# One form of score product for all 24 pairs of heads, and a remade order of tasks, in an attention and mixture-of-experts kernel

## The chip, the cores and the metric

The kernel runs on one core of one Trainium2 chip. Its time is the device time of one execution in microseconds (us), taken as the median of several runs. The core has a matrix engine (TensorE, in the rows PE, its weight loads PEld), a vector engine (VectorE, DVE), a scalar engine (ScalarE, ACT), a third elementwise engine (GpSimd, POOL) and a queue engine from which most transfers are started (SyncE, SP). Each engine works through its own instructions in the order in which they were written, and waits for the others by semaphores.

## What is computed

Four batches of 448 tokens with 12 heads of 64 columns pass through attention, a dense layer, and a layer of 8 experts of which each token takes one:

```python
q_n, k_n = rmsnorm(q, g_q), rmsnorm(k, g_k)
attn = softmax(q_n @ k_n.T / 8)             # per batch and head, 448 x 448
x = (attn @ v)                              # 1792 tokens x 768
x1 = square(maximum(x @ w_in, 0)) @ w_out   # 768 -> 2048 -> 768
e = argmax(x1 @ w_gate); p = softmax(x1 @ w_gate)[e]; o = sigmoid(x1 @ w_output_gate)[e]
out = p * o * (maximum(x1 @ w1[e], 0) @ w2[e])   # 768 -> 1024 -> 768
```

The inputs are float32. TensorE takes them as pairs of shorter numbers: each operand is split into a high and a low part, and a product a·b is made as high·high + high·low + low·high. Splitting costs one cast or scaled copy (the high part) and one subtraction (the low part) for each operand, on ACT, DVE or POOL.

## The kernel before

**Tiling.** The 12 heads of a batch are taken as 6 pairs. Four batches by six pairs are 24 pairs of heads, numbered b and p; in tile names `qk2_3_0` is tile 0 of batch 2, pair 3. A pair has 128 rows of head columns (64 for each head) and 448 tokens, cut into four chunks of 112.

**Steps of a pair.** `prepare` makes the normalised q and k (`nrm`, on POOL by L330 or on DVE by L331), transposes them on PE into PSUM (`qkps`, L576) and splits them into the tiles `qk`. `scores` makes for one chunk of queries both heads' scores (`sps`, PE), their negated maximum (`nm`, DVE, L664) and the exponential (`p`, ACT, L667). `turn` transposes the exponentials on PE (`pps`, L681), splits them (`pT`, ACT L317 and DVE L688) and multiplies with v (`av`, PE, L699 or L694). `combine` divides by the sum (`r`, `rb`, `rps`, L711 to L722) and joins the heads (`xs`, DVE, L732 and L734). When the six pairs of a batch are done their rows are split (`x`), and the first half of the dense layer can run for that batch: 16 blocks f of 18 products each (`hps`, L765), 288 products a batch. These 1152 products need only x and the weights `win`, so they fill PE between the attention steps of the next batches. The second half (`yps`, L1040), the routing (L1075 to L1258) and a first block of the first expert (L1343 to L1402) follow; from L1445 on the experts run in an order written out by hand.

**Two forms of scores.** For the first seven pairs (`halves`, L413, NHALF = 7) q and k are split over all 128 rows by four instructions of 128x448 (L583, L585, L589, L591), and a head's scores of a chunk are three products over its own 64 rows (L655), one task for each head. For the other 17 pairs each head's high and low part are stacked to 128 rows, which takes eight instructions of 64x448 (L599, L602 on ACT; L606, L610 on DVE) and two copies from one half of the rows to the other (kind `kd`, L317, L318 or L320), 5 tiles rather than 4; a chunk is then one 128-row product per head (L641, a task each) and one 64-row product per head (L649, one task for both).

**The order.** All of it up to L1442 is put down as tasks in a plan (class `Plan`, L84). A task has an engine, a cost, a priority, the buffers that it reads and writes, and perhaps other engines that may take it. `order` places tasks one after the other, by priority, into the first gap of their engine, with a latency between engines (`LAT`, L88), and the instructions are then written in the order of the planned starts. `ALT` (L243) says which other engines may take a kind of task, and at what addition to its priority and wait; `SHIFT` (L255) adds to the priorities of kinds of tasks. So a change of these numbers moves instructions on every engine, though none is added. PSUM has six banks for `qkps`, `sps`, `pps` and `rps` together (`Slots(6)`, L522), and there are eight places for the exponentials.

## Time and profile before

| | us |
|---|---|
| median of three runs | 1207.39 (1204.85 to 1207.52) |
| span of the profiled execution | 1204.1 |
| first score products of the kernel | 19.7 |
| first product of the dense layer (`hps`, batch 0) | 126.9 |
| last `av` product of batch 1 | 241.95 |
| last `av` product of batch 3 | 484.4 |
| last `hps` product | 578.3 |
| first product of the experts' hand-written part | 869.6 |

The profiled execution's span runs from its first to its last instruction; its own time is the span and the little that lies around it, and the median of the three runs is 3.3 us above the span. The mean granted clock of TensorE is 0.984 of full speed. PE is busy for 93% of the span, DVE 63%, ACT 51%, POOL 36%.

### The profile page before, as it was taken

To read this page: it belongs to the slowest core of one execution; us is meant where nothing else is said; L and a number is where in the kernel's file an instruction comes from. 1 tells how busy PE (TensorE), PEld (TensorE's weight loads), DVE (VectorE), ACT (ScalarE), POOL (GpSimd) and SP (SyncE) were. 2 spreads that over 40 slices of the span, in tenths; PEclk is the share of its full clock that TensorE was granted. 3 is DMA by queue.
4 is the path that set the end of the run, shared out by engine and by line. 5 is a ranking of instruction groups with operands and counts; after the bars stand their busy time and mean duration, and the time that the engine had idled before them with its cause. 6 is when DMAs were issued, how large, how long until landed. Compare 5 with 4: busy or idle time off the path is not lost.

```text
span 1204.1 us, 17242 instructions
## 1 busy us (share of the span) xinstructions
PE 1123.9 (93%) x6070; PEld 953.1 (79%) x6070; DVE 759.0 (63%) x1229; ACT 619.6 (51%) x1235; POOL 438.4 (36%) x437
## 2 busy tenths in 40 slices
PE   2999999999999999999999999999989878999997
PEld 2666777878777887998888989898879767897876
DVE  6999999968888688147787253443552566135662
ACT  4788878767776677234442222231252555133551
POOL 5657756575433431243222000013142444114431
PEclk9899999999999999999999999999999988999999
DMA  9933222233212110168533323273464486307601
GB/s 248 284 106 88 85 85 70 69 115 93 70 47 69 62 32 24 54 193 300 185 105 88 101 62 100 62 228 101 144 208 190 142 308 229 133 26 267 229 33 32
DMA packets 84755, 152.57 MB, mean 127 GB/s; under 512 B 10071, under 2 KB 63063, under 8 KB 84608
## 3 DMA queue, kind: packets, MB, share of 16 engines
q1 hardware_dynamic: 81152, 135.44, 36.0%
q0 software_dynamic: 3456, 15.34, 3.5%
q8 instruction: 71, 1.16, 0.4%
q14 instruction: 76, 0.62, 0.2%
HBM read 124.83 MB, written 26.79 MB: 126 GB/s over the span
## 4 chain that ended last, share of the span: by engine, by line
PE 63%; DVE 15%; issue 7%; ACT 6%; DMA 5%; POOL 2%; DVEq 0%; SPq 0%; POOLq 0%; ACTq 0%; another core or an unknown queue 0%
PE yps L1040 15%; PE hps L765 12%; PE hps L1486 9%; PE yps L1531 6%; PE av L699 5%; PE pps L681 4%; PE sps L641 2%; PE sps L649 2%; DVE w1hl L1503 2%; ACT w1hl L1501 2%; DVE pT L688 1%; DVE wout L325 1%; PE qkps L576 1%; DVE nm L664 1%; ACT wout L317 1%
## 5 line engine op out<-in xcount | busy, mean ns | idle before, releaser
L765 PE MATMUL hps<-x,win 128*128 128x448 f32 x1152 | 282.1, 377 | 0.9 <-ACT g L774 0.8
L1040 PE MATMUL yps<-gh,wout 128*128 128x448 f32 x1152 | 245.4, 368 | 2.8 <-ACT wout L317 2.4
L765 PEld LDWEIGHTS hps<-x,win 128*128 128x128 f32 x1152 | 211.7, 189 | 28.4 <-issue 11.1
L1040 PEld LDWEIGHTS yps<-gh,wout 128*128 128x128 f32 x1152 | 213.4, 188 | 22.7 <-ACT wout L317 2.8
L1486 PE MATMUL hps<-w1hl,xT 128*128 128x512 f32 x564 | 141.3, 400 | 14.2 <-DVE w1hl L1503 10.6
L1531 PE MATMUL yps<-w2hl,hT 128*128 128x384 f32 x752 | 144.0, 348 | 0.0
L667 ACT ACTIVATE p<-sps,nm 112x448 f32<-112x448 f32 x192 | 120.5, 635 | 35.5 <-DVE nm L664 34.0
L1486 PEld LDWEIGHTS hps<-w1hl,xT 128*128 128x128 f32 x564 | 103.7, 189 | 41.6 <-DVE w1hl L1503 15.4
L1531 PEld LDWEIGHTS yps<-w2hl,hT 128*128 128x128 f32 x752 | 134.4, 195 | 0.3 <-DVE hT L1479 0.2
L664 DVE TENSOR_REDUCE nm<-sps 112x1 f32<-112x448 f32 x192 | 111.6, 616 | 22.1 <-PE sps L649 20.0
L699 PE MATMUL av<-pT,v 112*128 112x448 f32 x356 | 116.1, 400 | 3.7 <-DVE pT L688 3.4
L688 DVE TENSOR_TENSOR pT<-pps,pT 112x448 fp32r<-112x448 f32 x178 | 105.3, 616 | 9.0 <-ACT pT L317 7.5
L317 ACT CAST pT<-pps 112x448 fp32r<-112x448 f32 x178 | 91.3, 535 | 27.4 <-PE av L699 13.3
L681 PE MATMUL pps<-ident,p 112*112 112x112 f32 x768 | 98.7, 264 | 5.4 <-DVE qk L606 1.6
L681 PEld LDWEIGHTS pps<-ident,p 112*112 112x112 f32 x768 | 82.7, 135 | 21.6 <-ACT p L667 3.3
L317 ACT CAST gh<-gr 128x448 fp32r<-128x448 f32 x64 | 36.1, 565 | 123.4 <-PE yps L1040 106.2
L330 POOL TENSOR_TENSOR g<-g 128x448 f32<-128x448 f32 x57 | 56.5, 991 | 114.8 <-ACT g L774 113.0
L325 DVE TENSOR_TENSOR gh<-gr,gh 128x448 fp32r<-128x448 f32 x64 | 44.6, 697 | 65.4 <-ACT gh L317 65.4
L699 PEld LDWEIGHTS av<-pT,v 112*128 112x128 f32 x356 | 60.6, 190 | 20.8 <-DVE pT L688 6.8
L1503 POOL TENSOR_TENSOR w1hl<-w1r,w1hl 128x1024 fp32r<-128x1024 f32 x14 | 38.2, 2728 | 96.7 <-ACT w1hl L1501 57.3
L1479 DVE TENSOR_TENSOR hT<-tps,hT 128x512 fp32r<-128x512 f32 x30 | 20.7, 690 | 72.4 <-ACT hT L1478 72.4
L330 POOL TENSOR_TENSOR nrm<-raw,rstd 112x512 f32<-112x512 f32 x47 | 51.8, 1123 | 37.2 <-PE qkps L576 27.5
(388 smaller groups left out, 1661.0 us busy)
## 6 DMA issues: line engine op xcount, KB each, us to landing
w2r<-in_moe_w_dram SPq DMA_DIRECT2D x64, 384.0 KB, 8.8
w1r<-in_moe_w_dram SPq DMA_DIRECT2D x42, 512.0 KB, 4.8
gscr<-g SPq DMA_DIRECT2D x64, 224.0 KB, 2.0
gr<-gscr SPq DMA_DIRECT2D x64, 224.0 KB, 2.6
raw<-in_q_dram SPq DMA_DIRECT2D x24, 224.0 KB, 3.1
raw<-in_k_dram SPq DMA_DIRECT2D x24, 224.0 KB, 3.4
vr<-in_v_dram SPq DMA_DIRECT2D x24, 224.0 KB, 2.7
x1s<-row SPq DMA_DIRECT2D x16, 336.0 KB, 3.0
```

Of the source, the lines that this page charges most:

```text
L317: (ACT, act(n, psum), lambda: nc.scalar.copy(dst(), src())),
L330: (POOL, pool(n), lambda: nc.gpsimd.tensor_mul(dst(), a(), b())),
L664: add(DVE, dve(S), pr + 1 + j, lambda j=j: nc.vector.tensor_reduce(nm()[:, j:j + 1], sp[j]()[:CP, :S], AX.X, ALU.max, negate=True), r=[sp[ ...
L667: add(ACT, act(S, True, 2), pr + 3 + j, lambda j=j: nc.scalar.activation(pt[j](), sp[j]()[:CP, :S], AF.Exp, bias=nm()[:, j:j + 1], accum_o ...
L681: nc.tensor.transpose(tp()[:CP, c * CP:(c + 1) * CP], pts[c][j]()[:, kc * CP:(kc + 1) * CP], ident[:CP, :CP])
L688: add(DVE, dve(S), pq + 2, lambda: nc.vector.tensor_sub(ht()[:, 1], tp()[:CP, :S], ht()[:, 0].bitcast(F32)), r=[tp, (ht, 0)], w=[(ht, 1)], ...
L699: add(PE, 187, pq + 3 + x, lambda x=x: nc.tensor.matmul(a_()[:, :S], vt()[:, j, kc, :], ht()[:, x, :], start=kc == 0 and x == 0, stop=kc = ...
L765: add(PE, 188, pr + n_, lambda d=d, x=x, y=y, n_=n_: nc.tensor.matmul(ps()[:, :S], w()[:, x, d * P:(d + 1) * P], x_t[b, d]()[:, y, :], sta ...
L1040: nc.tensor.matmul(ps()[:, :S], w()[:, x, d * P:(d + 1) * P], hl()[:, y], start=f == 0 and i == 0, stop=f == NFC - 1 and i == 2)
L1486: nc.tensor.matmul(hps[n], x, w1hl[d][:, y, n * 512:(n + 1) * 512], start=d == 0 and i == 0, stop=d == NCC - 1 and i == len(prods) - 1,)
L1503: e_.tensor_sub(w1hl[d][:, 1], w1r[d], w1hl[d][:, 0].bitcast(F32))
L1531: nc.tensor.matmul(yps[n][:, :NH], hT[f // HF][:, x, f % HF, :], w2hl[f][:, y, n * NH:(n + 1) * NH], start=f == 0 and i == 0, stop=f == NF ...
```

## The change

Three things change.

**Scores and splits.** All 24 pairs take the 64-row form. The chunk's six products become one task that names the two heads by turns; `halves`, L599 to L610 and the `kd` copies go. Lines move: L576 is L586 after, L583 to L591 are L593 to L601, L641, L649 and L655 are L634, L664 is L640, L667 is L643, L688 is L664, L765 is L741.

**The planner's numbers.** Costs of products go from 187 or 188 to 201 or 203, entering and leaving 64-row products costs 90 and 180, and most latencies change.

**The order.** ALT and SHIFT are replaced, so that tasks change their engine and place.

```diff
     LAT = {
-        (PE, ACT): 200, (PE, DVE): 60, (ACT, PE): 260, (ACT, DVE): 145, (ACT, POOL): 180,
-        (DVE, PE): 210, (DVE, ACT): 130, (DVE, POOL): 160, (POOL, PE): 210, (POOL, ACT): 80,
+        (PE, ACT): 210, (PE, DVE): 205, (ACT, PE): 175, (ACT, DVE): 135, (ACT, POOL): 180,
+        (DVE, PE): 150, (DVE, ACT): 125, (DVE, POOL): 170, (POOL, PE): 170, (POOL, ACT): 80,
...
+    HALF_IN, HALF_OUT = 90, 180
...
-                t["cost"] = clock.run(at, t["cost"], t["rows"])
+                extra = 0
+                if (t["rows"] == 64) != half:
+                    half = not half
+                    extra = self.HALF_IN if half else self.HALF_OUT
+                t["cost"] = clock.run(at, t["cost"], t["rows"]) + extra
...
 ALT = {
+    "norm": {DVE: (-1020, 500)},
...
 SHIFT = {
-    "combine_a": 200, "combine_a1": 3100, "combine_b": 6100, "combine_c": 300, "combine_c0": 1300,
+    "combine_a": 305, "combine_b": 8725, "combine_b1": -3320, "combine_c": 3365, "combine_c1": -12240,
...
-    NQK, NPT, DOUBLE, NHALF = 2, 3, False, 7
+    NQK, NPT, DOUBLE = 2, 3, False
...
-        hl = [new(A, f"qk{i}", NQK, [P, S], F32R, f"qk{b}_{p}_{i}") for i in range(5)]
+        hl = [new(A, f"qk{i}", NQK, [P, S], F32R, f"qk{b}_{p}_{i}") for i in range(4)]
...
-            for j in range(0 if halves(b, p) else 2):
-                add(PE, 187, pr + 0.1 * j, lambda j=j: nc.tensor.matmul(
-                    sp[j]()[:CP, :S], hl[j]()[:, cols], hl[2 + j](), start=True, stop=False),
-                    r=[(hl[j], 0), (hl[j], 1), (hl[2 + j], 0), (hl[2 + j], 1)],
-                    w=[sp[j], (pt[j], 1)], kind=f"scores_a{b}")
-
-            def low():
-                for j in range(2):
-                    own = slice(64 * j, 64 * j + 64)
-                    nc.tensor.matmul(
-                        sp[j]()[:CP, :S], hl[j]()[own, cols], hl[4]()[own], start=False, stop=True)
-
-            def mm(j):
-                own = slice(64 * j, 64 * j + 64)
+            def mm():
+
                 for i_, (x, y) in enumerate(((0, 2), (0, 3), (1, 2))):
-                    nc.tensor.matmul(
-                        sp[j]()[:CP, :S], hl[x]()[own, cols], hl[y]()[own], start=i_ == 0, stop=i_ == 2)
...
+                    for j in range(2):
+                        own = slice(64 * j, 64 * j + 64)
+                        nc.tensor.matmul(
+                            sp[j]()[:CP, :S], hl[x]()[own, cols], hl[y]()[own], start=i_ == 0, stop=i_ == 2)
+
+            add(PE, 600, pr, mm, r=[(hl[x], 0) for x in range(4)], w=sp + [(pt[j], 1) for j in range(2)],
+                rows=64, kind=f"scores_b{b}")
...
-                add(PE, 188, pr + n_, lambda d=d, x=x, y=y, n_=n_: nc.tensor.matmul(
+                add(PE, 203, pr + n_, lambda d=d, x=x, y=y, n_=n_: nc.tensor.matmul(
```

Counted over the attention part of the program (instructions before, after):

| instruction | before | after |
|---|---|---|
| PE score products | 440 | 576 |
| DVE `qk` splits of 64x448 / 128x448 | 68 / 14 | 0 / 48 |
| ACT `qk` splits of 64x448 / 128x448 | 68 / 14 | 0 / 48 |
| copies `qk<-qk`: DVE, ACT, POOL | 16, 10, 8 | 0, 0, 0 |
| `nrm` on DVE, POOL | 1, 47 | 11, 37 |
| `st` products on DVE, POOL | 0, 36 | 6, 30 |
| `v` subtractions on DVE, POOL | 5, 43 | 16, 32 |
| ReLU `g<-hps` on DVE, ACT | 0, 64 | 15, 49 |
| `hps` products ahead of the last `av` of batch 1, 2, 3 | 252, 473, 698 | 207, 406, 694 |
| score chunks behind the last `av` of batch 1 | 48 | 46 |

**Three places in the order.** First PE in the middle of the attention, chunk 1 of batch 2, pair 2 (`sps2_2_1_0` and `sps2_2_1_1` are the two heads' scores; `hps` are the dense layer's products, `x4` at a row's end that so many stand together). Before:

```order
L641 MATMUL sps2_2_0_0_3672<-qk2_2_2_3604,qk2_2_0_3485 112x448
L641 MATMUL sps2_2_1_0_3677<-qk2_2_2_3604,qk2_2_0_3485 112x448
L765 MATMUL hps1_4_3644<-x1_3_3149,win4_1588 128x448 x2
L765 MATMUL hps1_4_3644<-x1_4_3155,win4_1588 128x448 x3
L765 MATMUL hps1_4_3644<-x1_5_3169,win4_1588 128x448 x3
L641 MATMUL sps2_2_0_1_3696<-qk2_2_3_3612,qk2_2_1_3506 112x448
L649 MATMUL sps2_2_0_0_3672<-qk2_2_4_3630,qk2_2_0_3485 112x448
L649 MATMUL sps2_2_0_1_3696<-qk2_2_4_3630,qk2_2_1_3506 112x448
L641 MATMUL sps2_2_1_1_3703<-qk2_2_3_3612,qk2_2_1_3506 112x448
L649 MATMUL sps2_2_1_0_3677<-qk2_2_4_3630,qk2_2_0_3485 112x448
L649 MATMUL sps2_2_1_1_3703<-qk2_2_4_3630,qk2_2_1_3506 112x448
```

The same chunk of the changed kernel, on the same engine:

```order
L741 MATMUL hps1_0_3579<-x1_2_3505,win0_322 128x448
L634 MATMUL sps2_2_1_0_3615<-qk2_2_2_3176,qk2_2_0_3169 112x448
L634 MATMUL sps2_2_1_1_3617<-qk2_2_2_3176,qk2_2_0_3169 112x448
L634 MATMUL sps2_2_1_0_3615<-qk2_2_3_3186,qk2_2_0_3169 112x448
L634 MATMUL sps2_2_1_1_3617<-qk2_2_3_3186,qk2_2_0_3169 112x448
L634 MATMUL sps2_2_1_0_3615<-qk2_2_2_3176,qk2_2_1_3179 112x448
L634 MATMUL sps2_2_1_1_3617<-qk2_2_2_3176,qk2_2_1_3179 112x448
L741 MATMUL hps1_0_3579<-x1_2_3505,win0_322 128x448 x2
```

A chunk's products now stand in one block, and beside them block f = 0 of batch 1's dense layer instead of f = 4: at the same place of the attention 295 filling products have been written instead of 370.

Second DVE near its start, batch 0 (`win0g`, `win0r` are parts of the first weight unit). Before:

```order
L585 SCALAR_TENSOR_TENSOR qk0_1_1_327<-qkps0_1_0_304,gs_75,qk0_1_0_319 128x448
L325 TENSOR_TENSOR win0_300<-win0g_256,win0_300 128x768
L591 TENSOR_TENSOR qk0_1_3_354<-qkps0_1_1_313,qk0_1_2_329 128x448
L688 TENSOR_TENSOR pT0_0_0_0_344<-pps0_0_0_0_322,pT0_0_0_0_344 112x448
L711 TENSOR_SCALAR r0_0_374<-sum0_0_246 112x8
L712 RECIPROCAL r0_0_374<-r0_0_374 112x8
L664 TENSOR_REDUCE nm0_1_0_382<-sps0_1_0_0_370 112x1
```

The changed kernel on the same engine, at the same place:

```order
L347 TENSOR_TENSOR nrm0_1_294<-raw0_1_108,rstd0_154 112x2x4x64
L410 SCALAR_TENSOR_TENSOR win0g_279<-win0r_208,win0g_279 128x768
L458 TENSOR_REDUCE ss1_320<-st1_0_161 112x16
L664 TENSOR_TENSOR pT0_0_0_0_318<-pps0_0_0_0_304,pT0_0_0_0_318 112x448
L595 SCALAR_TENSOR_TENSOR qk0_1_1_344<-qkps0_1_0_312,gs_75,qk0_1_0_331 128x448
L601 TENSOR_TENSOR qk0_1_3_349<-qkps0_1_1_324,qk0_1_2_336 128x448
L687 TENSOR_SCALAR r0_0_361<-sum0_0_250 112x8
L688 RECIPROCAL r0_0_361<-r0_0_361 112x8
L595 SCALAR_TENSOR_TENSOR qk0_2_1_366<-qkps0_2_0_338,gs_75,qk0_2_0_352 128x448
L347 TENSOR_TENSOR nrm0_5_376<-raw0_5_135,rstd0_154 112x2x4x64
L601 TENSOR_TENSOR qk0_2_3_390<-qkps0_2_1_356,qk0_2_2_374 128x448
L347 TENSOR_TENSOR nrm0_5_376<-raw0_5_135,rstd0_154 112x2x4x64
```

Three normalisations stand on DVE that POOL had before; the low part of `win0` has gone from it, and pair 2's splits stand ahead of pair 1's first scores.

Third PE at the end of the planned part, the first expert's first block (`yps0`, `yps1` are its two halves of columns, `xps` the transposes of the next block's rows, `hps0` the next block's first products). Before:

```order
L1392 MATMUL yps0_9215<-w2hl4_8798,hT1_9247 128x384 x3
L1347 MATMUL xps_9007<-ident_68,w1r0_9225 128x128 x6
L1392 MATMUL yps0_9215<-w2hl5_8825,hT1_9247 128x384 x3
L1392 MATMUL yps0_9215<-w2hl6_8850,hT1_9247 128x384 x3
L1392 MATMUL yps0_9215<-w2hl7_8870,hT1_9247 128x384 x3
L1392 MATMUL yps1_9216<-w2hl4_8798,hT1_9247 128x384 x3
```

After:

```order
L1368 MATMUL yps1_9239<-w2hl4_8815,hT1_9231 128x384 x3
L1368 MATMUL yps1_9239<-w2hl5_8842,hT1_9231 128x384 x3
L1368 MATMUL yps1_9239<-w2hl6_8867,hT1_9231 128x384 x3
L1368 MATMUL yps1_9239<-w2hl7_8887,hT1_9231 128x384 x3
L1323 MATMUL xps_9026<-ident_68,w1r0_9252 128x128 x6
```

The six transposes have moved behind the last of the 48 `yps` products; the next block's `hps` products come directly behind them.

## Rows read from the trace of the kernel before

**Rows 1.** Windows: busy us of each engine (instructions), granted clock, DMA share, GB/s.

```profile
30.00:60.00 30.00, 28.47 (x153) 19.09 (x153) 27.89 (x44) 23.74 (x59) 19.06 (x19) 0.85 1.03 285
60.00:127.00 67.00, 63.16 (x395) 43.38 (x396) 65.41 (x117) 59.41 (x146) 43.72 (x53) 1.00 0.32 89
127.00:242.00 115.00, 111.53 (x632) 90.53 (x631) 111.30 (x175) 92.04 (x199) 70.17 (x69) 1.00 0.26 80
242.00:360.00 118.00, 113.48 (x651) 90.78 (x650) 95.39 (x164) 88.20 (x206) 60.31 (x82) 0.99 0.28 83
360.00:485.00 125.00, 122.59 (x720) 99.65 (x719) 98.71 (x170) 87.96 (x208) 41.17 (x50) 1.00 0.14 45
```

**Rows 2.** Chain of work that ended last, shares by line, 240 to 485 us.

```profile
by line: PE hps L765 37.1%; PE av L699 17.0%; PE pps L681 14.6%; PE sps L641 8.5%; PE sps L649 7.4%; PE qkps L576 3.0%; PE rps L722 1.9%; DVE qk L610 1.5%; issue 1.5%; DVE qk L318 1.4%; DVE nm L664 1.0%; POOL stt L499 0.7%; ACT xs L317 0.7%
```

**Rows 3.** Timeline of PE at two marks: start us, us, instruction.

```profile
126.94 0.37 PE L765 MATMUL hps<-x,win 128*128 128x448 f32 x1
...
241.95 0.78 PE L699 MATMUL av<-pT,v 112*128 112x448 f32 x3
```

**Rows 4.** Chain in order of time, score products and transposes on PE: start, us, piece.

```profile
41.88 0.80 PE sps L655 x6
...
44.02 0.79 PE sps L655 x3
...
65.05 1.42 PE sps L655 x12
...
251.03 0.41 PE sps L641 x2
...
252.26 0.39 PE rps L722 x4
...
253.89 0.38 PE sps L649 x2
```

**Rows 5.** Line 649, idle time of PEld before it: cause, us, times.

```profile
  issue: 20.4, 68
```

**Rows 6.** Groups of DVE: shapes, count | busy us, mean ns of one | idle before.

```profile
L606 DVE SCALAR_TENSOR_TENSOR qk<-qkps,gs,qk 64x448 fp32r<-64x448 f32 x34 | 23.2, 683 | 1.6 <-ACT qk L599 0.7
L448 DVE TENSOR_REDUCE ss<-st 112x16 f32<-112x1024 f32 x18 | 21.7, 1208 | 0.1
L610 DVE TENSOR_TENSOR qk<-qkps,qk 64x448 fp32r<-64x448 f32 x34 | 21.1, 619 | 1.3 <-ACT qk L602 0.4
L318 DVE CAST qk<-qk 64x448 fp32r<-64x448 f32 x16 | 13.9, 866 | 5.5 <-ACT qk L602 5.3
L585 DVE SCALAR_TENSOR_TENSOR qk<-qkps,gs,qk 128x448 fp32r<-128x448 f32 x7 | 4.7, 676 | 0.5 <-ACT qk L583 0.4
L591 DVE TENSOR_TENSOR qk<-qkps,qk 128x448 fp32r<-128x448 f32 x7 | 4.3, 612 | 1.1 <-ACT qk L589 1.1
```

**Rows 7.** Two products of 112x512 on DVE, and copies: ns min/median/max, first and last start.

```profile
L331 DVE TENSOR_TENSOR nrm<-raw,rstd x1: 1152/1152/1152, 14.0 to 14.0; 112x512 f32<-112x512 f32 x1
...
L331 DVE TENSOR_TENSOR sq<-raw x2: 681/686/692, 4.4 to 11.8; 112x512 f32<-112x512 f32 x2
...
L318 DVE CAST qk<-qk x16: 375/831/1575, 147.7 to 461.7; 64x448 fp32r<-64x448 f32 x16
```

**Rows 8.** Chain in order of time, a `nrm` on POOL: start us, us, piece.

```profile
13.59 1.05 POOL nrm L330
```

**Rows 9.** Waits of PE, 240 to 480 us: total us, times, longest.

```profile
PE qkps L576 <- POOL nrm L330: 2.7, 1, 2.7
PE sps L641 <- DVE qk L610: 1.8, 3, 0.6
```

**Rows 10.** Timeline of PE, ACT and DVE at the first expert's first block.

```profile
865.80 3.91 PE L1392 MATMUL yps<-w2hl,hT 128*128 128x384 f32 x21
...
866.13 0.80 ACT L1356 CAST xT<-xps 128x768 fp32r<-128x768 f32 x1 [4.31 <-PE xps L1347]
866.97 0.96 DVE L1357 TENSOR_TENSOR xT<-xps,xT 128x768 fp32r<-128x768 f32 x1 [4.43 <-ACT xT L1356]
```

More of the change, by code (lines that the diff above doesn't have):

```diff
@@ L102, in add @@
             "rows": rows, "lat": lat, "start": None,
-            "ways": ways or [(eng, cost, fn, 0, 0)], "kind": kind,
+            "ways": ways or [(eng, cost, fn, 0, 0)], "kind": kind, "base": base, "name": name, "every": every,
         }
@@ L128, in add @@
         t["deps"] = deps
-        t["bufs"] = {x[0] if isinstance(x, tuple) else x for x in list(r) + list(w)}
+        t["bufs"] = dict.fromkeys(x[0] if isinstance(x, tuple) else x for x in list(r) + list(w))
         t["bufs"] = [b for b in t["bufs"] if b.pool is not None]
@@ L143, in order @@
         free = [0.0] * 6
-        clock = Clock()
+        clock, half = Clock(), False
         def late(d, eng):
@@ L243 @@
 ALT = {
-    "g2": {ACT: (200, 3000)},
+    "g2": {ACT: (1000, 300), DVE: (300, 100)},
+    "gH": {DVE: (20, 200), POOL: (1100, 200)},
     "kd": {ACT: (0, 1500), POOL: (0, 200)},
-    "q0": {DVE: (0, 800)},
-    "vH": {POOL: (1000, 200)},
-    "vL": {DVE: (-100, 400)},
-    "wL": {DVE: (0, 800)},
-    "xL": {DVE: (200, 200)},
-    "yH": {DVE: (0, 0)},
-    "yL1": {DVE: (-100, 0)},
+    "norm": {DVE: (-1020, 500)},
+    "oL": {POOL: (-1000, 200)},
+    "q0": {POOL: (-4280, 900)},
+    "relu": {DVE: (0, 300)},
@@ L253 @@
+    "sq": {DVE: (540, 0)},
+    "vH": {DVE: (-320, 5200), POOL: (-1700, 100)},
+    "vL": {DVE: (780, 200)},
+    "wH": {DVE: (20, 400)},
+    "wL": {DVE: (-200, 1100)},
+    "xH": {DVE: (-20, 200)},
+    "xL": {DVE: (1100, 600)},
+    "y": {ACT: (-1000, 200)},
+    "yH": {DVE: (900, 400)},
+    "yL1": {DVE: (-880, 100)},
 }
 SHIFT = {
-    "combine_a": 200, "combine_a1": 3100, "combine_b": 6100, "combine_c": 300, "combine_c0": 1300,
-    "combine_d0": 5900, "combine_d1": 4300, "combine_e0": 205, "combine_e1": 10300, "load_qk_pair_a": -3100,
@@ L604, in prepare @@
[L604 to L614 removed]
+            add(PE, 381, pr - 200 + a, tr, r=[(nrm, a)], w=[ps] + [(x, 1) for x in hl[2 * a:2 * a + 2]], rows=CP, kind=f"prepare_d{b}")
```

89 lines of the change are left out of this document (31 added, 58 removed).

## The prediction, made before the changed kernel ran

> **What bounds the kernel now.** I read the windows by stage first [rows 1]. From 60 us on PE is never idle for long, but neither is DVE: it is busy 65.4 of 67 us between 60 and 127, and 111.3 of 115 between 127 and 242, while PE has 3.8 and 3.5 us to spare. From 242 on DVE falls to 95.4 of 118 and 98.7 of 125, and PE is the engine that is full. The chain of waits says the same of the later stretch: between 240 and 485 us some 90% of it lies on PE, 37.1% on the filling products of the dense layer [rows 2]. So there are two regimes. Through batches 0 and 1 both engines are tight, DVE the tighter; behind 242 us an instruction taken from DVE or ACT gives nothing unless PE waits for it, and the end moves by PE's work and PE's waits. Two marks cut the time: the first filler at 126.94, which needs the last row of batch 0's x from DVE, and the last `av` of batch 1 at 241.95 [rows 3]. I sum the shift of the second mark, and what follows it on PE.
>
> **The score products on PE.** Six 64-row products, three of each head, take 0.80 us in the chain even where the old code names one head's three and then the other's; three of a lone head take 0.79; twelve take 1.42 [rows 4]. So two heads already run side by side, and taking them by turns saves nothing by itself. What it removes is the lone visit: before the first filler the old order has 18 runs of score products, 5 of them of three; the new one has 20 of six, two of twelve and one of 24. At 0.79 to 0.80 up to six and 0.62 more for each further six (1.42 - 0.80), that is 2.2 us less PE work ahead of the first filler, by my count over the two orders, the odd runs put between their neighbours. For the other 17 pairs a chunk was two 128-row products (0.41 as a pair) and two 64-row ones (0.38) [rows 4], together 0.79; now it is 0.80. The 68 chunks cost the same, except that ten runs are of twelve, each 0.18 shorter (-1.8 us). PEld waited 20.4 us in 68 visits, 0.30 each, at the entry into 64 rows [rows 5]; ten visits fewer are worth up to 3.0 us, of which I take 1.0.
>
> **Up to the first filler (mark 126.94).** DVE gets five more `nrm`, two `st` and two `v` ahead of the row that opens the fillers. One `nrm` on DVE took 1.15 us; a product of the same 112x512 without a second tensor took 0.69 [rows 7]. The 1.15 one ran from 14.0, beside a POOL `nrm` of 13.59 to 14.64 [rows 8]: the high price is that of a DVE instruction with POOL at work, and POOL is busy 43.7 of 67 us [rows 1]. Five cost 3.4 to 5.8 us; the other moves cancel nearly (two `st` and two `v` against three `pT` and two weight instructions that are written later: -0.8). DVE's list is 2.7 to 5.0 us longer. Against it: 2.1 us of DVE idleness between 30 and 60 and 1.6 from 60 to 127 [rows 1], the 2.2 us of PE, and splits that are written earlier, as the order near the start shows. I take -0.5 us, with -4 and +4 as ends.
>
> **Batch 1 (126.94 to 241.95).** Between the two marks DVE loses ten 64-row pairs of splits and gains six full-width ones: a full-width one costs no more than a 64-row one, 0.676 and 0.612 against 0.683 and 0.619 [rows 6]. That is -13.0 + 7.7, and three copies of 0.87 go: -7.9 in all. It gains five `nrm` (+3.4 to +5.8), four statistics sums of batch 2 that are pulled forward, 1.21 each [rows 6] (+4.8), three `st` at 0.69 (+2.1), and two `nm` and three `pT` which lay on the other side of a mark (+3.1). The sum is +5.5 to +7.9 us. Where does it go? DVE's idle 3.7 us of this window [rows 1] can take part of it; POOL has some 15 us less work by the end of batch 1, and DVE's own copies ran from 0.375 to 1.575 us [rows 7], so that some of the instructions that POOL slows now come faster. I charge +1.5 us to the second mark, ends -3 and +7. This is the number I trust least. Filling products are no cover here: in the order 207 of them stand ahead of that mark instead of 252, so that PE has less to do while DVE finishes.
>
> On the price of `nrm` the Trainium skill speaks against the change: "SBUF — State Buffer", section "SBUF: two separate sides", says that DVE and GpSimd share one pair of ports by an exclusive lock held for a whole instruction, a DVE instruction with two SBUF inputs contending with a GpSimd one that reads SBUF. By that rule all ten `nrm` would tend to the upper price. The one such overlap in this trace agrees with it [rows 7, 8].
>
> **PE's work behind the second mark.** The 45 fillers that weren't placed come later: 45 at 0.205, half of the pair's 0.41 [rows 4], hence +9.2. Against them stand two chunks that are already done (-1.6), 16 fewer transposes of q and k and four of `rps` at 0.1, four having taken 0.39 [rows 4] (-2.0), and the joined runs and entries (-2.8): +2.8. Fewer waits between visits could take another 1 to 2; I take +1.5, ends 0 and +4.
>
> **PE's waits behind it.** PE is idle 4.5 us between 242 and 360 and 2.4 between 360 and 485 [rows 1]. The largest piece is 2.7 us for a POOL `nrm` of batch 2, whose statistics ended late; then waits for splits, 1.8 [rows 9]. After the change batch 2's statistics are complete before batch 1's last `pT`, its first `nrm` is partly on DVE ahead of it, and four splits take the place of eight and the copies (0.87 each, with 5.5 us of idle time before them for ACT's part [rows 6]). The scores of a chunk now ask for two banks and two places at once, which before could be taken one after the other: a new wait, with the fillers behind it on PE. I take -6 for waits and for the small losses between visits that no row shows singly, ends -9 and 0.
>
> **The end of the plan.** Transposes for the next block used to stand with 21 products, 3.91 us, behind them, and ACT's 0.80 and DVE's 0.96 hid there [rows 10]. Now they stand last and nothing hides the two copies: +1.8 at full price. I take +1.5, as the gather before them might be waited for less. The second dense half, the routing and the hand-written experts keep their work; I put them at 0, with 2 either way.
>
> **Sum.** -0.5 + 1.5 + 1.5 - 6 + 1.5 = -2.0. Against the profiled span of 1204.1 that is 1202.1; the median of the runs lies 3.3 above the span, so 1205.4. A measurement of this kernel can tell about 0.3%, 3.6 us, from no change.
>
> **Rivals.** *DVE is relieved, and both tight batches shorten.* With POOL lighter by 15 us up to the end of batch 1 and 31 up to the end of batch 2, DVE's shared instructions come near their lowest prices, the new nrm's near 0.69. First mark -4, second -4 more, PE's work +1.5, waits -7, end +1.5: -12, 1195. For it speaks the spread of the copies; against it, that most DVE instructions there read PSUM, and `nm` and the splits cost the same throughout.
>
> *DVE becomes the one bound through batch 1, and the time is worse.* The `nrm` cost 1.15 each, batch 2's statistics come forward, and DVE's list up to the last `pT` of batch 1 is 5.0 + 7.9 = 12.9 us longer. It decides from the point where this exceeds the idle time of DVE, 1.6 + 3.7 us. The second mark moves by 7.6 (all idle time used) to 12.9 us (none), say 9.5; PE waits there for `pT`, and the 45 fillers, which could have filled it, stand behind it in PE's order and are paid later. With +1.5 for them, -3 for waits behind and +1.8: +9.8, 1217. DVE's 97% between 60 and 242 speaks for it; that PE, too, has less to do up to the mark takes nothing from it.
>
> *The change does nothing at PE.* Two heads side by side were there before [rows 4], the stacked form cost as much, and the order only exchanges one set of waits for another: 0, 1207.
>
> **How the numbers follow.** The forecast has 0.42, the relieved DVE 0.22, the bound DVE 0.23, nothing gained 0.13. The forecast's own spread puts 0.15 of its 0.42 below -3.6 us and 0.05 above +3.6, so faster is 0.22 + 0.15 + 0.03 for a deeper cut of the waits in the last case, 0.40; slower 0.23 + 0.05 = 0.28 with same 0.32. The ends of the terms, added, give -18 and +19; all ends on one side are unlikely, and the range goes to just past the two rivals, 1191 to 1218.
>
> **What the profile after would show.** First filler within 123 to 131 us; last `av` of batch 1 between 239 and 249. If DVE in 60 to 240 us is 99% busy and that mark lies past 249, the slow rival holds; before 236, the fast one. The `nrm` on DVE: near 0.7 or 1.15. Between the mark and the last filler, PE idle under 4 us and no wait for POOL `nrm`. At the end, about 1.8 us of PE idleness ahead of the next block's first product. A score chunk of six should take 0.80 and a pair of chunks 1.42. The forecast is wrong if the waits behind 242 don't fall, or if the experts' part changes length by more than 2 us.

## The result, and the profile after

The changed kernel takes 1213.38 us (median of six runs, 1210.61 to 1216.78) against 1207.37 of the kernel before beside it. The ratio is 1.0062, 95% interval 1.0046 to 1.0078: slower by 6 us by the medians and by 7.5 by the ratio, where 2 us faster was forecast. One of the six executions of the kernel before was a slow one, 1261.47, and the ratio leaves it out. The profiled span went from 1204.1 to 1211.2, +7.1 us. By marks (starts, us):

| mark | before | after | shift | forecast shift |
|---|---|---|---|---|
| first filler (`hps`) | 126.9 | 129.9 | +3.0 | -0.5 |
| last `av` of batch 1 | 241.95 | 252.0 | +10.1 | +1.0 |
| last `av` of batch 3 | 484.4 | 488.4 | +4.0 | |
| last `hps` | 578.3 | 584.4 | +6.1 | -3.5 |
| end of the span | 1204.1 | 1211.2 | +7.1 | -2.0 |

So 10.1 us are lost by the second mark, 4.0 come back up to the last filler, and 1.0 goes behind it. The windows of the changed kernel, with the columns of [rows 1] and a slice behind the first mark:

```profile
30.00:60.00 30.00, 26.78 (x143) 18.21 (x144) 29.28 (x45) 21.45 (x53) 18.52 (x17) 0.80 0.90 269
60.00:127.00 67.00, 59.46 (x370) 38.20 (x367) 65.57 (x117) 55.95 (x138) 37.04 (x47) 1.00 0.38 106
127.00:242.00 115.00, 107.81 (x636) 81.45 (x636) 109.80 (x173) 85.27 (x195) 68.99 (x64) 0.97 0.30 91
242.00:360.00 118.00, 116.17 (x748) 94.35 (x747) 97.70 (x179) 81.95 (x199) 49.39 (x58) 1.00 0.23 71
360.00:485.00 125.00, 123.51 (x764) 102.65 (x764) 79.82 (x144) 74.07 (x184) 35.41 (x42) 1.00 0.13 43
130.00:140.00 10.00, 7.40 (x22) 3.04 (x21) 9.18 (x13) 5.83 (x12) 4.87 (x5) 0.71 0.37 93
```

Against [rows 1], PE has 9.1 us less busy time between 30 and 242 (1.7, 3.7 and 3.7 by window) and 3.6 more from 242 to 485. DVE is as full as before in the tight stretches (65.6 of 67, 109.8 of 115) and nearly without a pause between 30 and 60 (29.3 of 30, before 27.9). A bad slice stands right behind the first mark: from 130 to 140 PE is busy 7.4 of 10 us. The timeline of PE and DVE there (start, us, instruction, idle time ahead of it and its releaser):

```profile
131.59 0.59 PE L657 MATMUL pps<-ident,p 112*112 112x112 f32 x4 [1.18 <-DVE qk L595]
131.99 2.27 DVE L347 TENSOR_TENSOR nrm<-raw,rstd 112x512 f32<-112x512 f32 x1
134.18 0.61 DVE L664 TENSOR_TENSOR pT<-pps,pT 112x448 fp32r<-112x448 f32 x1
134.85 1.46 PE L634 MATMUL sps<-qk,qk 64*112 64x448 f32 x5 [1.31 <-DVE pT L664]
```

PE waits 1.31 us for a `pT` of DVE, and ahead of that `pT` DVE had a `nrm` for 2.27 us. The wait has an echo: five score products take 1.46 us, and the next six 1.24, where six take 0.79 at full clock (both in the chain shown under experiment 2). The granted clock of the slice is 0.71, so part of it ran at the lower of the two levels (1.2 GHz) behind PE's idle time. For these two blocks alone that is some 1.1 us (1.46 + 1.24 - 2 x 0.80) beside the wait, an estimate.

The shape group answers the disputed price. `nrm` on DVE, mean and total beside the full-width splits (count | busy us, mean ns | idle before):

```profile
L595 DVE SCALAR_TENSOR_TENSOR qk<-qkps,gs,qk 128x448 fp32r<-128x448 f32 x24 | 16.2, 676 | 4.0 <-ACT qk L593 4.0
L347 DVE TENSOR_TENSOR nrm<-raw,rstd 112x512 f32<-112x512 f32 x11 | 16.2, 1471 | 0.3 <-POOL rstd L511 0.3
L601 DVE TENSOR_TENSOR qk<-qkps,qk 128x448 fp32r<-128x448 f32 x24 | 14.7, 613 | 1.9 <-ACT qk L599 1.9
```

The splits cost what [rows 6] said, 0.676 and 0.613. A `nrm` costs 1.47 on the mean, above the 1.15 that I took from [rows 7] as the upper end. Its spread, and that of the moved `st` and `v` (ns min/median/max, first and last start):

```profile
L347 DVE TENSOR_TENSOR nrm<-raw,rstd x11: 692/1155/3767, 16.3 to 218.7; 112x512 f32<-112x512 f32 x11
L347 DVE TENSOR_TENSOR st<-st x6: 682/840/1296, 23.0 to 263.5; 112x512 f32<-112x512 f32 x6
L341 DVE TENSOR_TENSOR v<-vr,v x16: 406/426/955, 21.5 to 459.6; 112x256 fp32r<-112x256 f32 x16
```

**What sets a `nrm`'s time** stands in the timelines of DVE and POOL, read side by side. DVE:

```profile
39.84 3.77 DVE L347 TENSOR_TENSOR nrm<-raw,rstd 112x512 f32<-112x512 f32 x1
...
92.74 1.94 DVE L347 TENSOR_TENSOR nrm<-raw,rstd 112x512 f32<-112x512 f32 x1
...
174.48 1.01 DVE L347 TENSOR_TENSOR nrm<-raw,rstd 112x512 f32<-112x512 f32 x1
...
203.79 0.69 DVE L347 TENSOR_TENSOR nrm<-raw,rstd 112x512 f32<-112x512 f32 x1 [0.34 <-POOL rstd L511]
```

And POOL at the same times:

```profile
39.22 2.06 POOL L346 TENSOR_TENSOR st<-st 112x512 f32<-112x512 f32 x2 [0.39 <-issue]
41.24 1.82 POOL L340 TENSOR_TENSOR win<-win0g,win 128x768 fp32r<-128x768 f32 x1
...
92.98 1.16 POOL L340 TENSOR_TENSOR x<-xs,x 128x448 fp32r<-128x448 f32 x1
...
131.90 1.81 POOL L340 TENSOR_TENSOR win<-win4g,win 128x768 fp32r<-128x768 f32 x1
...
173.90 1.04 POOL L346 TENSOR_TENSOR nrm<-raw,rstd 112x512 f32<-112x512 f32 x1 [1.42 <-issue]
...
203.84 1.55 POOL L346 TENSOR_TENSOR nrm<-raw,rstd 112x512 f32<-112x512 f32 x1
```

Take the ends: DVE's `nrm` of 39.84 ends at 43.61, POOL's `win` at 43.06, 0.55 earlier. The one of 92.74 ends at 94.68, POOL's `x` at 94.14; the one of 131.99 at 134.26, `win` at 133.71; the one of 174.48 at 175.49, POOL's `nrm` at 174.94. Each time 0.54 or 0.55. The one of 203.79 began in a gap of POOL's and took 0.69, and there it was POOL's `nrm` that took 1.55 for its usual 1.04. Of all eleven, ten end 0.54 to 0.56 us behind the end of a POOL instruction. So a `nrm` on DVE costs what is left of POOL's work plus some 0.55 us; the one at 39.84 waited for the end of three POOL instructions in a row, two of which began after it. A row's start is thus where DVE began to wait, and a long row is mostly a wait. The 1.15 of [rows 7, 8] was no upper price: POOL's `nrm` there ended at 14.64, DVE's at 15.15. The Trainium skill's "SBUF — State Buffer", section "SBUF: two separate sides", has the rule, an exclusive lock held for a whole instruction, between a DVE instruction with two SBUF inputs and a GpSimd one that reads SBUF; these rows agree with it.

### The profile page after: what moved, and what is told of

The parts are those of the page before. It is cut to its first block, busy times and chain, and to the rows that moved or that the text cites. A ratio compares the mean times of both kernels' runs of the same rounds, so it can differ in the third digit from the quotient of the medians.

```text
span 1211.2 us, 17363 instructions
## 1 busy us (share of the span) xinstructions
PE 1121.7 (93%) x6206; PEld 943.5 (78%) x6206; DVE 734.6 (61%) x1202; ACT 593.7 (49%) x1200; POOL 418.4 (35%) x397
## 4 chain that ended last, share of the span: by engine, by line
PE 60%; DVE 16%; ACT 7%; issue 7%; DMA 4%; POOL 3%; DVEq 0%; SPq 0%; ACTq 0%; POOLq 0%
PE yps L1016 14%; PE hps L741 12%; PE hps L1462 9%; PE yps L1507 6%; PE av L675 5%; PE pps L657 4%; PE sps L634 4%; ACT w1hl L1477 2%; DVE w1hl L1479 2%; DVE nm L640 2%; DMA w1st<-in_moe_w_dram 1%; PE tps L1447 1%; DVE gh L341 1%; ACT wout L333 1%; PE qkps L586 1%
## 5 line engine op out<-in xcount | busy, mean ns | idle before, releaser
L741 PE MATMUL hps<-x,win 128*128 128x448 f32 x1152 | 266.7, 372 | 1.7 <-ACT g L750 1.1
L741 PEld LDWEIGHTS hps<-x,win 128*128 128x128 f32 x1152 | 211.3, 188 | 26.5 <-issue 8.0
L643 ACT ACTIVATE p<-sps,nm 112x448 f32<-112x448 f32 x192 | 120.7, 636 | 50.7 <-DVE nm L640 50.4
L675 PE MATMUL av<-pT,v 112*128 112x448 f32 x356 | 120.0, 412 | 5.8 <-DVE pT L664 3.2
L640 DVE TENSOR_REDUCE nm<-sps 112x1 f32<-112x448 f32 x192 | 109.4, 615 | 18.2 <-PE sps L634 17.3
L664 DVE TENSOR_TENSOR pT<-pps,pT 112x448 fp32r<-112x448 f32 x178 | 104.6, 617 | 14.4 <-ACT pT L333 13.6
L346 POOL TENSOR_TENSOR g<-g 128x448 f32<-128x448 f32 x50 | 50.0, 1001 | 145.2 <-ACT g L750 112.1
L634 PE MATMUL sps<-qk,qk 64*112 64x448 f32 x576 | 85.6, 403 | 6.5 <-ACT qk L593 3.1
L333 ACT CAST gh<-gr 128x448 fp32r<-128x448 f32 x58 | 32.7, 565 | 112.5 <-PE yps L1016 108.9
L634 PEld LDWEIGHTS sps<-qk,qk 64*112 64x112 f32 x576 | 47.9, 179 | 35.8 <-issue 11.8
```

Of the source, the lines that this page charges most:

```text
L333: (ACT, act(n, psum), lambda: nc.scalar.copy(dst(), src())),
L634: nc.tensor.matmul(sp[j]()[:CP, :S], hl[x]()[own, cols], hl[y]()[own], start=i_ == 0, stop=i_ == 2)
L640: add(DVE, dve(S), pr + 1 + j, lambda j=j: nc.vector.tensor_reduce(nm()[:, j:j + 1], sp[j]()[:CP, :S], AX.X, ALU.max, negate=True), r=[sp[ ...
L643: add(ACT, act(S, True, 2), pr + 3 + j, lambda j=j: nc.scalar.activation(pt[j](), sp[j]()[:CP, :S], AF.Exp, bias=nm()[:, j:j + 1], accum_o ...
L664: add(DVE, dve(S), pq + 2, lambda: nc.vector.tensor_sub(ht()[:, 1], tp()[:CP, :S], ht()[:, 0].bitcast(F32)), r=[tp, (ht, 0)], w=[(ht, 1)], ...
L675: add(PE, 201, pq + 3 + x, lambda x=x: nc.tensor.matmul(a_()[:, :S], vt()[:, j, kc, :], ht()[:, x, :], start=kc == 0 and x == 0, stop=kc = ...
```

## The experiments

All ratios are to the kernel before, run beside each. The changed kernel stands at 1.0062.

**1. The ten `nrm` given back to POOL, and put on DVE in the old order.** In the changed kernel the order is kept (they are planned on DVE) and only the engine that they are issued to changes:

```diff
+            if not first:
+                ways[1] = (DVE, ways[1][1], ways[0][2])
```

> The changed kernel with its order kept; only the ten normalisations that the new tables had given to DVE are issued to POOL, at the same place. Theory A (price of those ten on DVE, 16.2 us for 11 in the trace of the changed kernel, up to 3.8 us for one, where 0.7 to 1.15 was assumed): DVE's list up to batch 1's last pT is 14 us shorter, the last av of batch 1 comes near 244 instead of 252.5, and the time falls by 5 to 9 us, to 1204 to 1208. Theory B (the rest of the new order is at fault, the normalisations are only along for the ride): the mark stays past 249 and the time falls by less than 2 us.

Measured: 1210.75, ratio 1.0038 [1.0018, 1.0058], 2.6 us below the changed kernel, less than the 5 to 9 of Theory A and at the edge of what the two intervals can tell apart. The first filler comes at 127.32, 2.6 us earlier, but the last `av` of batch 1 only at 251.19 (the changed kernel 252.0), where Theory A wanted 244: what batch 0 gains, batch 1 loses again. The slice behind the first mark is healed and another one opens; windows of this run:

```profile
130.00:140.00 10.00, 9.60 (x52) 5.91 (x51) 9.74 (x16) 6.04 (x15) 7.08 (x6) 1.00 0.46 116
190.00:215.00 25.00, 22.59 (x119) 17.25 (x117) 21.39 (x34) 16.32 (x37) 16.73 (x22) 0.86 0.29 88
```

The changed kernel has PE busy 23.45 of 25 us at a granted clock of 1.00 between 190 and 215. Here the `nrm` stand on POOL behind the statistics (`stt`, `rstd`), and PE waits 1.99 us in one piece (from ACT's `pT`) with a lower clock behind it.

The reverse, the kernel before with the same ten on DVE in place:

```diff
+            if (b, p, a) in ((0, 1, 1), (0, 5, 0), (0, 5, 1), (1, 0, 1), (1, 2, 1), ...):
+                ways[0] = (POOL, 1000, ways[1][2])
```

> The kernel before with its order kept; ten normalisations of the same pairs (one of each of 0_1, 1_0, 1_2 to 1_5, 2_0, 2_1, both of 0_5) are issued to DVE instead of POOL, at the same place. Theory A: they take 1.2 to 1.6 us each, the last av of batch 1 comes 6 to 11 us later than 242, and the time rises by 4 to 8 us. Theory B: DVE finds room for them, the time rises by less than 2 us.

Measured: 1209.49, 1.0019 [1.0003, 1.0034], 2.6 us above its reference, where 4 to 8 were expected; the first filler comes 4.7 us later (131.68) and the last `av` of batch 1 7.1 (249.02). The two runs agree in size and sign. In this order the same ten cost DVE far less:

```profile
L331 DVE TENSOR_TENSOR nrm<-raw,rstd x11: 673/705/1523, 15.4 to 257.2; 112x512 f32<-112x512 f32 x11
```

So the price is not the instruction's but the place's: a median of 0.705 in this order, 1.155 in the new one. All eleven take 10.5 us of DVE here and 16.2 there, and yet the time changes by the same 2.6 us; so DVE's price of the `nrm` doesn't by itself tell what they cost at the end.

**2. By turns or head after head.** The changed kernel with each head's three products in a row:

```diff
-                for i_, (x, y) in enumerate(((0, 2), (0, 3), (1, 2))):
-                    for j in range(2):
-                        own = slice(64 * j, 64 * j + 64)
+                for j in range(2):
+                    own = slice(64 * j, 64 * j + 64)
+                    for i_, (x, y) in enumerate(((0, 2), (0, 3), (1, 2))):
```

> The changed kernel with a chunk's six score products written head after head (three of one, then three of the other) instead of by turns; nothing else moves. Theory A and the prediction: two heads run side by side either way, a block of six takes 0.80 us, the time stays within 2 us of the changed kernel. Theory C (turns matter): each of the 96 chunks costs up to 0.4 us more, in the tight stretches that is 10 us and more.

Measured: 1213.7, 1.0054 [1.0037, 1.0072]: the same as the changed kernel. A chunk of six in its chain of waits, in order of time (start, us):

```profile
70.43 0.80 PE sps L634 x6
```

And in the changed kernel's:

```profile
71.61 0.79 PE sps L634 x6
...
140.16 1.24 PE sps L634 x6
```

**3. The score form without the remade order.** The kernel before with the 64-row form and full-width splits in all 24 pairs, its numbers and tables kept. It also takes over one line of the changed kernel that keeps a task's buffers in written order (`dict.fromkeys`); that line alone was not run.

```diff
-        return b * NPR + p < NHALF
+        return True
...
-                for j in range(2):
-                    add(PE, 565, pr + 0.1 * j, lambda j=j: mm(j), ...)
+                add(PE, 600, pr, mm, ..., w=sp + [(pt[j], 1) for j in range(2)], rows=64, ...)
```

> The form of scores and splits alone: the kernel before with all 24 pairs in the 64-row form by turns, with the old costs, latencies and tables (the 17 other pairs keep their old additions to the priority). Theory A: DVE keeps only one normalisation and is 8 us lighter in batch 1, the last av of batch 1 comes 0 to 5 us earlier and the time is 0 to 8 us under the kernel before. Theory C (the new form costs PE more than it saves): slower than before by 3 us or more.

Measured: 1203.62, 0.9964 [0.9947, 0.9981]. The first filler comes late, at 138.67, yet PE has no gap from 242 to 485. In this run the transposes also wait for a free place of their split tiles. Then the same, but with the first seven pairs left as they were (a task for each head, no such wait), so that the order up to batch 1 should be that of the kernel before (first filler at 128.57 for 126.94):

```diff
+                if b * NPR + p < NHALF:
+                    for j in range(2):
+                        add(PE, 565, pr + 0.1 * j, lambda j=j: mm((j,)), ..., w=[sp[j], (pt[j], 1)], ...)
```

> As the run with the form alone (old costs, latencies and tables), but the first seven pairs keep their old tasks, one for each head, so that the order up to the start of batch 1 is that of the kernel before; only the other 17 pairs take the new form by turns. Theory A (the form saves waits behind 250 us, the order decides what happens before): first filler at 127 (the form alone had 138.7), PE waits behind 250 us of 2 us in all as in that run, where the kernel before has 9; the time is 1196 to 1201. Rival: the smooth flow behind 250 us of that run came only from its late start; then the waits return and the time is 1203 or more.

Measured: 1193.66, 0.9874 [0.9847, 0.9901]: 14 us faster than the kernel before and 20 faster than the changed one, and better than the 1196 to 1201 expected. Its windows:

```profile
127.00:242.00 115.00, 113.68 (x708) 93.09 (x706) 109.94 (x175) 88.61 (x199) 85.72 (x76) 1.00 0.34 101
242.00:360.00 118.00, 115.65 (x718) 92.11 (x718) 92.76 (x158) 82.36 (x198) 54.48 (x70) 0.97 0.23 69
360.00:485.00 125.00, 125.00 (x767) 103.61 (x767) 75.32 (x134) 77.15 (x187) 35.34 (x42) 1.00 0.13 43
```

PE is busy 113.7 of 115 us in batch 1 (before 111.5, after 107.8) and 125.0 of 125 from 360 to 485. Here POOL has 85.7 us of work in batch 1, 17 more than in the changed kernel, which took work off it. Between 127 us and its last filler at 568.3 PE is idle for 4.4 us, in the kernel before (to 578.3) for 11.3, with 437 us of work for 440. So with the old numbers and tables the new form can come out 14 us ahead, and the changed kernel loses 20 against that by its order. The 14 us are the form's together with the order that the planner makes of it: the same form in all 24 pairs gave 0.9964 above, and 1.0070 in experiment 6.

**4. What of the order costs it: work moved to DVE.** The changed kernel with the ten `nrm`, the six `st` and the 16 `v` subtractions back on POOL, in place (`nrm` by the edit of experiment 1; planned on DVE, issued to POOL):

```diff
+            sq[2] = (DVE, sq[2][1], sq[1][2])
...
+            lows[1] = (DVE, lows[1][1], lows[0][2])
```

> As the run with the ten normalisations on POOL, and DVE's six squares (st) and its v subtractions go to POOL too, each at its place. Theory A (what the tables moved to DVE is the loss): 5 to 8 us under the changed kernel, twice the gain of the ten normalisations alone. Theory B: POOL, in order, is then late itself, as in that run at 194 to 206 us, and the time is that of the run with ten normalisations, 1209 to 1212.

Measured: 1203.14, 0.9974 [0.9952, 0.9996]: 10.2 us below the changed kernel, more than the 5 to 8 of Theory A. Its windows (the profiled execution took 1199.31, 3.8 us below this run's median, so that they flatter it):

```profile
30.00:60.00 30.00, 29.31 (x173) 20.33 (x174) 26.52 (x47) 23.52 (x56) 21.83 (x22) 1.00 1.03 295
60.00:127.00 67.00, 60.16 (x372) 38.53 (x371) 64.92 (x113) 58.71 (x144) 45.43 (x53) 0.99 0.34 97
127.00:242.00 115.00, 110.49 (x672) 86.13 (x673) 105.91 (x172) 86.61 (x196) 79.66 (x73) 0.99 0.33 95
```

DVE has 2.8, 0.7 and 3.9 us less in the three windows, and PE 2.5, 0.7 and 2.7 more; between 30 and 60 the granted clock is 1.00 instead of 0.80. The first filler comes at 121.85, 8.1 us earlier than in the changed kernel, and DVE's work up to it falls from 115.3 to 105.6 us. The last `av` of batch 1 comes at 240.24: batch 1 takes 118.4 us, where the changed kernel takes 122.1 and the kernel before 115.0. So of the 7.1 us lost in batch 1, 3.7 come back with the work and 3.4 don't. Then the kinds apart, only the six `st` and only the 16 `v`:

> The changed kernel with its order kept; only DVE's six squares (st, five of them ahead of batch 1's end) go to POOL. The three kinds together gave 10.2 us, the ten normalisations alone 2.6. If the kinds add up, squares and v together give 7.6, and the squares, which run beside the POOL square of the same pair, 2 to 5 of it: 1208 to 1211. If the gain is in the overlap (DVE and POOL each free of the other only when all have moved), each kind alone gives under 3: 1210.5 or more.

> The changed kernel with its order kept; only DVE's 16 v subtractions go to POOL (four of them stand ahead of the first filler, eleven behind batch 1, where DVE is not tight). If the kinds add up: 1208 to 1211. If the gain is in the overlap: 1211 or more. In any case little should come from the eleven late ones.

Measured: 1209.50, 1.0023 [1.0000, 1.0045], and 1216.39, 1.0071 [1.0041, 1.0101]. So `st` gives 3.9, `nrm` 2.6, and `v` nothing that shows (3 us the wrong way, its interval covering the changed kernel's ratio). Together they give 10.2. Whether they simply add can't be told: by the intervals each of these differences is uncertain by 3 to 4 us. Last, the other direction, experiment 3's best kernel with ten `nrm`, six `st` and 14 `v` more on DVE in place (20 `v` in its trace, 6 without the moves):

> The best run so far (old order up to batch 1, new form behind it; 1193.7) with the same kinds of work moved to DVE at their places: the ten normalisations, six squares and 13 v subtractions more. Theory A (these moves are the loss, in whichever order): slower by 6 to 11 us, 1200 to 1205. Rival (only the new order is sensitive to them): within 3 us of 1193.7.

Measured: 1209.64, 1.0031 [1.0003, 1.0059], 16 us above the same kernel without the moves (19 by the ratios), more than the 6 to 11 expected. The loss begins early. The first fillers and the last blocks of 18, PE's timeline of this kernel:

```profile
139.68 0.45 PE L777 MATMUL hps<-x,win 128*128 128x448 f32 x1
...
582.03 3.91 PE L777 MATMUL hps<-x,win 128*128 128x448 f32 x18 [0.36 <-ACT g L786]
```

And of the kernel without the moves:

```profile
128.57 0.46 PE L771 MATMUL hps<-x,win 128*128 128x448 f32 x1
...
564.63 3.91 PE L771 MATMUL hps<-x,win 128*128 128x448 f32 x18 [0.36 <-ACT g L780]
```

11.1 us are lost by the first filler, 17.4 by the last block. The `nrm` in it have a median of only 0.693, though single `v` took up to 3.64 beside POOL. DVE's work up to the first filler grows from 112.2 to 120.8 us, 8.5 of the 11.1, and PE's waits for `pT` of DVE between 60 and 140 us from 2.7 to 6.9. Not all of it is DVE's list: PE's one wait for POOL's first `nrm` is 5.8 us where it was 3.8 in two, and DVE itself waits 1.7 us for a `v` of POOL that waited for its load. That moves of this kind cost 10 us in one order and 16 in the other is shown.

**5. Rivals on the order.** The changed kernel planned with a true price of a `nrm` on DVE, so that the planner could place it otherwise:

```diff
+            ways[1] = (DVE, 1470, ways[1][2])
```

> The changed kernel with one number of the planner changed: a normalisation on DVE is planned at 1470 ns, its mean in the trace, instead of 602; the order follows from that, and 6 of the 10 go back to POOL or elsewhere by the planner's own choice. Theory A (the planner filled DVE with work at less than half its price and wrote fillers too late): 248 fillers stand ahead of batch 1's last av instead of 207, PE loses 5 us less between 100 and 150 us, the time falls by 3 to 8 us against the changed kernel, to 1205 to 1210. Rival (the tables' other moves are at fault): within 2 us of the changed kernel.

Measured: 1222.35, 1.0133 [1.0109, 1.0158]. A truer cost made the order worse by 9 us, where 3 to 8 better was expected; that the tables suit the untrue one would explain it and is not shown. Then one half of the remade order at a time, the old tables with the new numbers, and the new tables with the old numbers:

```diff
-    "norm": {DVE: (-1020, 500)},
...
+    "xL": {DVE: (200, 200)},
...
-    "combine_a": 305, "combine_b": 8725, "combine_b1": -3320, "combine_c": 3365, "combine_c1": -12240,
+    "combine_a": 200, "combine_a1": 3100, "combine_b": 6100, "combine_c": 300, "combine_c0": 1300,
```

> The changed kernel with the old ALT and SHIFT tables (the 17 pairs' splits and scores with the additions that their old kinds had), and the new costs and latencies. If the new tables are at fault: near the run with the form alone, 1200 to 1207. If the new costs and latencies are: 1210 or more.

```diff
-    HALF_IN, HALF_OUT = 90, 180
+    HALF_IN, HALF_OUT = 0, 0
...
-                add(PE, 4 * 201, pq + 3, lambda: nc.tensor.matmul(
+                add(PE, 4 * 187, pq + 3, lambda: nc.tensor.matmul(
```

> The changed kernel with its new ALT and SHIFT tables, but the old costs of products, the old latencies and no cost for entering and leaving 64-row products. If the new tables are at fault: 1211 or more. If the new costs and latencies are: 1201 to 1208.

Measured: 1229.78, 1.0191 [1.0167, 1.0216], and 1219.93, 1.0116 [1.0080, 1.0152]. Either half with the other's old one is worse than the pair: numbers and tables belong together, and these runs can't say which half loses the time.

The prediction also feared the fillers that stand behind the mark. In this run the fillers of batch 0 are written up to 5 us of the plan earlier:

```diff
+            if t["kind"] == "mlp_h_a0":
+                k = max([k - 5000] + [...its dependences...])
```

> The changed kernel; after planning, the filling products of batch 0 are written up to 5 us (of the plan's time) earlier in PE's order, as far as their inputs are planned to be there; all else keeps its order. 34 instead of 18 of them stand ahead of the last av of batch 1's first pair, 227 instead of 207 ahead of batch 1's last. Theory B (the new order writes the fillers too late, so that PE waits for attention steps while fillers stand behind): PE loses 3 to 6 us less between 127 and 242 us, the time falls by 3 to 6 us against the changed kernel. Theory A (DVE's list is too long there, fillers only push the attention back): within 2 us.

Measured: 1231.63, 1.0210 [1.0182, 1.0238]. PE's busy time falls to 104.6 of 115 us in batch 1 and 110.8 of 118 behind it: as I read it, a filler ahead of an attention step delays the step, and with it the engines that feed on it. That earlier fillers would have helped PE falls, as far as those of batch 0 go.

**6. Two changes to the best kernel.** With the chunk's joint task in the first seven pairs too:

```diff
-                if b * NPR + p < NHALF:
-                    for j in range(2):
-                        add(PE, 565, pr + 0.1 * j, lambda j=j: mm((j,)), ..., w=[sp[j], (pt[j], 1)], ...)
-                else:
+                if True:
                     add(PE, 600, pr, mm, ..., w=sp + [(pt[j], 1) for j in range(2)], rows=64, ...)
```

> As the best run so far (old order up to batch 1, new form behind it), but the first seven pairs' scores are one task for both heads by turns, with the old tables; without the wait of the transposes for the ring, which the run with the form alone had besides. If the joint task delays batch 0 (its two banks and two places must be free at once): first filler near 138 and 1201 to 1205, as with the form alone. If the ring's wait did it: first filler near 128 and 1192 to 1196.

Measured: 1214.92, 1.0070 [1.0045, 1.0095]; the first filler comes at 145.20. That is 21 us worse than with a task for each head, under the old tables, and outside both forecasts. It is also 11 us worse than the first run of experiment 3, from which it differs only by the transposes' wait in those seven pairs: here a small change of tasks, through the planner, moves the time by some 10 us. The second change concerns the one long wait that this kernel has left behind 240. DVE's timeline there, and PE's:

```profile
252.26 6.28 DVE L325 TENSOR_TENSOR x<-xs,x 128x448 fp32r<-128x448 f32 x4
258.46 1.67 DVE L694 TENSOR_TENSOR pT<-pps,pT 112x448 fp32r<-112x448 f32 x3
...
259.12 1.86 PE L705 MATMUL av<-pT,v 112*128 112x448 f32 x4 [2.35 <-DVE pT L694]
```

Four `x` take 6.28 us, 1.57 each where one alone took 0.62, beside POOL work without a pause from 251.20 to 257.96; again DVE ends 0.58 behind it. Those of batch 1's pairs from the third on went to POOL; one of these was there already, so three moved:

```diff
+        if b == 1 and p >= 2:
+            lows[1] = (DVE, lows[1][1], lows[0][2])
```

> As the best run so far, but four low parts of x of batch 1, which took 6.3 us in a row on DVE beside POOL and held up a pT for 2.35 us of PE's time, are issued to POOL at the same place. Expected: that wait goes, 2 to 4 us under the best run, 1190 to 1192; rival: the x come later from POOL and the fillers of batch 1 wait, no gain.

Measured: 1194.25, 0.9890 [0.9868, 0.9913]: no gain. The wait of 2.35 us is gone, but a longer one stands in its place, for an `x` that had stayed on DVE. DVE's timeline of this run, POOL's, and PE's:

```profile
254.01 6.32 DVE L325 TENSOR_TENSOR x<-xs,x 128x448 fp32r<-128x448 f32 x1
...
257.63 2.21 POOL L324 TENSOR_TENSOR x<-xs,x 128x448 fp32r<-128x448 f32 x2
...
260.38 1.28 PE L773 MATMUL hps<-x,win 128*128 128x448 f32 x5 [3.42 <-DVE x L325]
```

POOL, with three more `x`, runs without a pause from 252.03 to 262.12, and this single `x` of DVE takes 6.32 us, its end 0.49 behind the end of POOL's last. So the run doesn't tell what the wait was worth; it shows that what stays on DVE can pay for what is added to POOL beside it.

## Why the prediction was wrong

**The regimes** were read rightly: up to 242 us what DVE must do moves the marks, behind it PE's work and waits do. The windows of experiment 4 show it (DVE 2.8 and 3.9 us less, PE 2.5 and 2.7 more).

**The two shifts** are the terms that were mis-sized: -0.5 measured +3.0, +1.5 measured +7.1. The step that failed is the one by which DVE's idle time, PE's lighter work and cheaper shared instructions were to take up a list that I had priced at +2.7 to +5.0 and +5.5 to +7.9 us. Windows up to the first mark and between the marks, before and after in turn (columns of [rows 1]):

```profile
0.00:126.90 126.90, 100.02 (x583) 68.81 (x584) 111.94 (x198) 97.60 (x232) 78.55 (x103) 0.96 0.64 173
0.00:129.90 129.90, 95.41 (x560) 62.59 (x560) 115.26 (x201) 95.31 (x227) 70.46 (x93) 0.95 0.63 174
126.94:241.95 115.01, 111.54 (x631) 90.54 (x630) 111.31 (x175) 92.10 (x199) 70.18 (x69) 1.00 0.26 80
129.94:252.02 122.08, 115.27 (x683) 87.19 (x681) 116.94 (x185) 89.20 (x201) 72.90 (x67) 0.97 0.30 89
```

DVE's work grew by 3.3 us up to the first mark and by 5.6 between the marks, both inside what I had priced. Its idle time did not pay for any of it: 15.0 and 14.6 us up to the first mark, 3.7 and 5.1 between them. So the marks moved by the whole list, and between the marks by 1.4 us more. The measured +10.1 lies inside the slow rival's 7.6 to 12.9, and past the 249 us that I gave as its sign; DVE's share between 60 and 242 us didn't rise to the 99% that I wanted to see with it (96.4%, before 97.1%).

**The price of `nrm`** failed too. I took 0.69 to 1.15 from [rows 7, 8] as ends. The eleven took 16.2 us, the ten new ones 15.0, against 6.9 to 11.5; the five ahead of the first filler took 8.8 of that, the five of batch 1 6.3, against 3.4 to 5.8 each. The row of 1.15 was a product that had waited for 0.6 us of a POOL instruction; the right bound was the rest of POOL's run, up to 3.2 us here, plus 0.55. That DVE's whole list came out as priced all the same is luck: its other items must have cost less than I had put down.

**Behind the mark** the sum held, +1.5 and -6 against a measured -4.0, but by luck, as neither term did. Windows from each second mark to the last filler, before and after:

```profile
242.00:578.30 336.30, 328.45 (x1819) 274.66 (x1818) 235.67 (x386) 208.38 (x466) 132.15 (x167) 0.99 0.31 101
252.00:584.40 332.40, 327.68 (x1930) 278.07 (x1929) 215.50 (x367) 183.01 (x422) 110.14 (x131) 1.00 0.29 95
```

PE's idle time fell by 3.1 us (7.9 to 4.7), not 6, and its work by 0.8 instead of rising by 1.5. The 2.7 us wait for POOL's `nrm` [rows 9] is gone, and the largest is 1.1 in total (`hps` for ACT's `g`, four times). The 4.7 us are a little over the 4 that I named. **The end of the plan** cost about 1.0 for +1.5; PE's timeline has the bare copies, 0.89 and 0.26 us of waiting where I wrote 1.8 at full price:

```profile
877.03 0.82 PE L1323 MATMUL xps<-ident,w1r 128*128 128x128 f32 x6
878.73 0.74 PE L1462 MATMUL hps<-w1hl,xT 128*128 128x512 f32 x2 [0.89 <-ACT xT L1332]
879.72 2.60 PE L1462 MATMUL hps<-w1hl,xT 128*128 128x512 f32 x10 [0.26 <-DVE xT L1333]
```

**The score form** was right in what it denied (turns save nothing, experiment 2; a chunk 0.79 to 0.80), and it lacked a term for what the form can give in another order: 14 us in experiment 3. That run's windows show where: from 242 to 485 DVE has 168.1 us of work and ACT 159.5, against 194.1 and 176.2 in [rows 1], and PE is idle 2.4 us there for 6.9.

**The relieved DVE** fell: POOL was 5.4 us lighter up to the second mark (143.4 against 148.7, the sums of the windows above), not some 15, and no relief shows in DVE's work.

**What stays open.** Of the 20 us between the changed kernel and the best one, 10.2 are the work moved to DVE. The other 9 or 10 are not separated, and neither are the 3.4 us of batch 1 that stay when the work is moved back. The joint task in batch 0 costs 21 us under the old tables, but experiments that change tasks remake the whole order, and the new tables were not run with a task for each head. Whether `nrm`, `st` and `v` give back more together than apart is open too.
